# Attention and two feed-forward layers in one kernel: another order for the first loads and the first weight conversions

## The chip, the cores and the metric

The kernel runs on one core of one Trainium2 chip. The metric is the time of one execution on the device in microseconds (us). The kernel before was run three times: 1001.72 us in the median, 1000.77 to 1002.63.

## What is computed

There are N = 6016 tokens of C = 256 channels. The attention works across channels: queries and keys are normalised over the token axis, the scores are a 256 x 256 matrix summed over all tokens, and the softmax of it is applied to the values. Two feed-forward layers with DFF = 2048 follow.

```python
qn = q / (np.linalg.norm(q, axis=1, keepdims=True) + 1e-06)
kn = k / (np.linalg.norm(k, axis=1, keepdims=True) + 1e-06)
s = kn.transpose(0, 2, 1) @ qn / tau
a = softmax(s)
x = (v @ a).reshape(N, C)
h = x @ w_in1;  x = (relu(h) ** 2) @ w_out1
h = x @ w_in2;  out = np.maximum(0.01 * h, h) @ w_out2
```

So all of q and k has to be read before the softmax, and nothing of the feed-forward layers can start until the softmax is there.

## The kernel before

**The head (lines 237 to 507).** The 47 tiles of 128 tokens form 12 blocks (`tiles`, line 237): blocks 0 to 10 have four tiles, block 11 has three. `load_qk(n)` (line 331) loads one block of q and one of k into one buffer of five (`AHEAD`, line 240); `PIECES` (line 238) says in how many pieces: block 0 in four, blocks 1 to 3 in two, the others in one. All loads are issued by SyncE's queue (SP), except the keys of block 0, which ScalarE's queue issues (line 338).

The loop over the blocks (line 365) does this for block n, and each engine takes its own part in the order in which the lines stand, since the head runs under a manual schedule (line 322):

- ScalarE squares the block (line 371), then takes what lies in its list of later steps (line 374); after block 11 it also loads a table (line 373).
- VectorE adds the squares to `acc` (line 376). After block 11 it reduces `acc` to `sums_` (lines 378 to 380). Then it takes its list of later steps (line 381).
- TensorE multiplies q and k into the scores `sT` (line 386), 16 rows of the trace for a block of four tiles. Before the last two tiles it runs `norm_sums` (line 384), matmuls that read `sums_` and write `pn`.
- `run(steps[0], ...)` (line 393) takes steps of a weight conversion, and the next block, n + 5, is loaded (line 395).

After the loop the softmax follows: square roots of `pn` (line 437), small VectorE operations (440 to 446), scaling and transposing the scores (450 to 459), maxima and exponentials (470 to 474), transposes (478). TensorE multiplies the result into the first block of `w_in1` (`fold(0)`, line 497), and the first layer begins (line 704).

**A weight conversion.** A weight arrives as a 512 KB block of 64-bit words (`Unit.load`, line 131, three buffers `wst`). `converted` (line 294) turns it into a high and a low float: `scaled` (ScalarE, line 143), `shifted`, `sign`, `high` (VectorE, lines 146, 149, 153), `round` (ScalarE, line 192), `low` (VectorE, line 110). The first `next` puts `scaled` into ScalarE's list; each of the next three issues one VectorE step; the last of them puts `round` into ScalarE's list, and `low` goes to VectorE's list one block later.

In the kernel before, `first_i[0]` (block 0 of `w_in1`) is loaded behind block 3 (line 343) and converted around blocks 2 to 4 (`STEPS`, line 354). `first_i[1]` is loaded behind block 11 (line 397) and converted between the loop and the softmax (lines 433 to 452). `first_o` (block 0 of `w_out1`) is loaded behind the values and `tau` (line 401), and its conversion is a task of the plan below.

**The rest (lines 510 to 1913).** Everything behind the softmax is a list of tasks with costs and due times. `build` makes the tasks, `simulate` orders them with a model of the engines, and the plan whose TensorE ends first is written out. `convert` (line 1021) makes the tasks of a weight conversion; `CONV_BEGIN, CONV_END` (line 881) bound the stretch in which the weights of the second layer are converted; `FOLD_AFTER` (line 883) says behind which product of a unit the fold of the next one stands. The first four units of the first layer have a fixed order on TensorE (`PLAIN`, line 518).

Of the kernel before, what the change touches and what calls it, by code (L numbers as in the profile page):

```python
# [28 lines left out]
def attn_moe_moe2(  # L29
# [12 lines left out]
    nc = tc.nc  # L42
# [3 lines left out]
    T = N // P  # L46
# [188 lines left out]


    tiles = [(t0, min(G, T - t0)) for t0 in range(0, T, G)]
    PIECES = {0: ((0, 1), (1, 1), (2, 1), (3, 1)), **{n: ((0, 2), (2, 2)) for n in (1, 2, 3)}}
    NS = len(tiles)
    AHEAD = 5  # L240
    sT = [bank("ab"[j], f"sT{j}") for j in range(KC)]
# [52 lines left out]
    def converted(units):  # L294

        for u in units:
            later[ACT].append(u.scaled)
            yield
            for step in (u.shifted, u.sign, u.high):
                step()  # L300
                if step == u.high:
                    later[ACT].append(u.round)
                    later[ACT].append(lambda u=u: later[DVE].append(u.low))
                yield

    def run(steps, n):
        for _ in range(n):
            next(steps, None)

    first_i = [Unit("i", 1, g) for g in range(2)]  # L310
    first_o = Unit("o", 1, 0)
    others = [Unit(kind, 1, g) for k in range(1, NG) for kind, g in (("i", k + 1), ("o", k)) if g < NG]
    with (
# [17 lines left out]
        def load_qk(n):  # L331
            t = qk[n] = att4.tile([P, 2, G, C], F32, tag="qk", name="qk")
            for i, m in pieces(n):

                t0 = (tiles[n][0] + i) * P
                for a, x in enumerate((q, k)):
                    src = x[0][t0 : t0 + m * P, :].rearrange("(p g) c -> p g c", g=m)
                    (nc.scalar if a and n == 0 else nc.sync).dma_start(t[:, a, i : i + m], src)  # L338

        for n in range(AHEAD):  # L340
            load_qk(n)
            if n == 3:
                first_i[0].load()
        tiny = small[:, 6, 0:1]
        nc.vector.memset(tiny, 1e-36)
        nc.scalar.activation(small[:, 7, 0:1], ones, AF.Square)
# [2 lines left out]

        for _ in range(6):  # L350
            nc.tensor.matmul(warm[:, :P], zeros, zeros, start=True, stop=True)
        steps = [converted([u]) for u in first_i]

        STEPS = {2: 1, 3: 3}

        def norm_sums():

# [7 lines left out]
        for n, (t0, g) in enumerate(tiles):  # L365
            t = qk.pop(n)
            last_tile = n == NS - 1

            sq = att2.tile([P, 2, G, C], F32, tag="sq", name="sq") if n else acc
            for i, m in pieces(n):  # L370
                nc.scalar.activation(part(sq, i, m), part(t, i, m), AF.Square)
            if last_tile:
                nc.scalar.activation(small[:, 7, 0:1], ones, AF.Sqrt)
            flush(ACT)
            if n:
                tt(part(acc, 0, g), part(acc, 0, g), part(sq, 0, g), op=ALU.add)
            if last_tile:
                tt(part(acc, 0, 2), part(acc, 0, 2), part(acc, 2, 2), op=ALU.add)
                tt(sums_[:, :C], acc[:, 0, 0], acc[:, 0, 1], op=ALU.add)
                tt(ordered(sums_[:, C:]), in_order(acc[:, 1, 0]), in_order(acc[:, 1, 1]), op=ALU.add)  # L380
            flush(DVE)
            for i in range(g):
                if last_tile and i == g - 2:
                    norm_sums()
                for j in range(KC):
                    nc.tensor.matmul(  # L386
                        sT[j][:, :C],
                        t[:, 0, i, j * P : (j + 1) * P],
                        t[:, 1, i],
                        start=n == 0 and i == 0,  # L390
                        stop=last_tile and i == g - 1,
                    )
            run(steps[0], STEPS.get(n, 0))
            if n + AHEAD < NS:
                load_qk(n + AHEAD)
            elif n + AHEAD == NS:
                first_i[1].load()
                load_first_v(0)
                load_first_v(1)
                nc.sync.dma_start(tau_sb, tau.partition_broadcast(P))  # L400
                first_o.load()
                others[0].load()

        xa, xb = x_tile(2, 1, 0), x_tile(1, 1, 0)

# [24 lines left out]

        nc.vector.reciprocal(rtau, tau_sb)

        run(steps[1], 1)
        flush(ACT)
        run(steps[1], 2)
        y, m, z, r = (small[:, i] for i in range(4))
        nc.scalar.activation(y, pn[:, :4], AF.Sqrt, bias=tiny, scale=0.25)
        nc.scalar.activation(small[:, 7, 0:1], ones, AF.Exp)
# [10 lines left out]
        sTs = [att.tile([P, C], F32, name=f"sTs{j}") for j in range(KC)]  # L449
        ts(ordered(sTs[0]), in_order(sT[0][:, :C]), r[:, 0:1], rtau, op0=ALU.mult, op1=ALU.mult)  # L450
        nc.scalar.activation(ordered(sTs[1]), in_order(sT[1][:, :C]), AF.Copy, scale=rq1)
        run(steps[1], 1)
        others[1].load()
        s = [bank("e", "s0"), bank("y3", "s1")]
        x_transpose(0, 0, "y1")
        x_transpose(1, 0, "y2", range(2))
# [421 lines left out]
    TAIL = 12  # L878
    TURNS = 14
    FIRST_MIXED = min([p for L, p in GROUPS if L == 1], default=0)  # L880
    CONV_BEGIN, CONV_END = 1.4, 4
    N0 = 4
    FOLD_AFTER = "F1"
    LOAD = 22
    VDUE = 30, 60
    SEED_GAPS = 1, 0
# [100 lines left out]
    def build(base):  # L987
# [6 lines left out]
        wi_b, wo_b, x_b, g_b, c_b, o_b, v_b = {}, {}, {}, {}, {}, {}, {}  # L994
        low_of, x_ready = {}, {}
        wi_ready, wo_ready = {}, {}
        stores = {}
        y_after = {}

        def T(*a, **k):  # L1000
            return Task(*a, **k)
# [15 lines left out]
        wst_b = {i: Buf("wst", 3, i - 10) for i in range(3)}  # L1017
# [3 lines left out]
        def convert(u, due, loaded=None, first=None, pace=4, begin=0):  # L1021
            L, g = u.L, u.g
            d = lambda i: due + i * pace
            blocks = u.blocks
            if loaded is None:
                w = Buf("wst", 3, d(-12))
                t = T("SP", "wst", d(-12), u.load, alloc=w, lat=LOAD, deps=[begin] if begin else (),
                      release=d(-12) - 60 if begin else 0)
                deps = [t]
            else:  # L1030
                w, deps = loaded, ()
            cm = Buf("cm", 2, d(0))
            t = T("ACT", 3.2, d(0), u.scaled, deps=deps, alloc=cm, uses=[w])
            t = T("DVE", 1.9, d(1), u.shifted, deps=[t], uses=[cm])
            t = T("DVE", 3, d(2), u.sign, deps=[t], uses=[w, cm])
            if blocks:
                raw_ = Buf("whl", 2, d(4))
                t = T("DVE", 3, d(4), u.high, deps=[t], alloc=raw_, uses=[w, cm])
                for i in range(4):
                    t = T("DVE", 1.1, d(4.2 + i / 10), lambda i=i: (sums if u.kind == "i" else out_sums)(u.x)[i](),  # L1040
                          deps=[t], uses=[raw_])
                to = Buf("wis", 1, d(5))
                t = T("ACT", 4.6, d(5), u.round, deps=[t], alloc=to, uses=[raw_])
                t = T("DVE", 5.2, d(6), u.low, deps=[t], uses=[raw_, to])
            else:
                t = T("DVE", 3, d(4), u.high, deps=[t], uses=[w, cm])
                if (u.kind, L) == ("o", 1):
                    to = wo_b[1, 0, g] = Buf("wo", 4, d(5))
                elif u.kind == "i":
                    to = whl_b[g] = Buf("whl", 2, d(5))  # L1050
                else:
                    to = Buf("whl", 2, d(5))
                t = T("ACT", 2.7, d(5), u.round, deps=[t], alloc=to, uses=[cm])
                t = T("DVE", 3, d(6), u.low, deps=[t], uses=[cm, to])
            if u.kind == "o" or L == 2:
                stores[u.kind, L, g] = T("SP", "wo" if L == 1 else "wi" if u.kind == "i" else "store", d(7), u.store, deps=[t], uses=[to], lat=LOAD)
            return t

        whl_done = {0: None, 1: None}
        for i, u in enumerate([first_o, *others]):  # L1060
            n = u.g - 1 if u.kind == "i" else u.g + 1
            m, at0 = in_pair0(n)
            due = at0(m["fold"] if u.kind == "i" else m["second"][u.g > 0][0])
            t = convert(u, due - 35 - (0 if i else 10), loaded=wst_b.get(i))
            if u.kind == "i":
                whl_done[u.g] = t
            else:
                wo_ready[1, 0, u.g] = t
# [36 lines left out]
        for n in range(N0):  # L1105
            L, p, g = units[n]
            w = WIDTH[p]
            m, at0 = in_pair0(n)
            if g + 1 == N0 < NG:
                fixed.append(fold_sums(n, at0(m["fold"])))  # L1110
            elif g + 1 < NG:
                pw = {}
                b = wi_b[1, 0, g + 1] = Buf("wi", 3, at0(m["fold"]))
                t = T("PE", 6.4, at0(m["fold"]), lambda g=g, pw=pw: pw.update(enumerate(fold(g + 1))),
                      deps=[whl_done[g + 1], *pw_after], alloc=b, uses=[whl_b[g + 1], eT_b])
# [12 lines left out]
            for i, (half, fb) in enumerate(((0, 0), (0, 1), (1, 0), (1, 1))):  # L1128
                tag = "abe"[(4 * n + i) % 3]
                if (n, i) == (0, 0):  # L1130
                    t = T("PE", 12, at0(0), plain_first_both, n, "ab", uses=[wi])
                    fixed.append(t)
                elif (n, i) != (0, 1):
                    t = T("PE", 6, at0(m["first"][i]), plain_first, n, half, fb, tag,
                          deps=[*bank_after.get(tag, ()), wi_ready[1, 0, g]], uses=[wi])
# [5 lines left out]
            for half in range(2):  # L1141
# [4 lines left out]
                t = T("ACT", 4.6, at0(m["cast"][half]), nonlinear, n, half, w, "cast", deps=[t], uses=[c], alloc=b)  # L1146
# [797 lines left out]
```

## Time and profile before

| what | value |
|---|---|
| median of three runs | 1001.72 us (1000.77 to 1002.63) |
| the profiled execution | 1002.93 us |
| its span, first to last instruction | 1001.1 us |
| TensorE (PE) busy | 994.6 us, 99% of the span |
| VectorE (DVE) busy | 901.4 us, 90% |
| ScalarE (ACT) busy | 804.4 us, 80% |
| DMA | 234.97 MB, mean 235 GB/s |

The profiled execution is one run of its own: it took 1.8 us more than its span, and 1.2 us more than the median of the runs. Times in the rows below are microseconds from the start of the span.

### The profile page before, as it was taken

What the parts mean: (1) busy time and instruction counts of PE and PEld (TensorE: products, weight loads), DVE (VectorE), ACT (ScalarE), POOL (GpSimd) and SP (SyncE); (2) the same over time, 40 slices, a digit from 0 to 9 for tenths busy, and PEclk for the clock granted to TensorE, in tenths of its full rate; (3) what the DMA queues carried; (4) which work ended last, traced back from release to release, by engine and by line L of the source; (5) the groups of instructions that cost most, each with busy time, mean ns of one, the idle gap of its engine ahead of it and who ended that gap; (6) DMA issues with size and microseconds to landing.
All of it is one profiled execution on the core that took longest, in us unless ns stands there. A gap on an engine that the chain in (4) does not pass through costs nothing.

```text
span 1001.1 us, 13148 instructions
## 1 busy us (share of the span) xinstructions
PE 994.6 (99%) x4528; PEld 837.3 (84%) x4528; DVE 901.4 (90%) x1314; ACT 804.4 (80%) x1184; POOL 0.7 (0%) x6
## 2 busy tenths in 40 slices
PE   9999999999999999999999999999999999999998
PEld 7888888887888888998888888888888888998887
DVE  4899999988988977999999999999999999998985
ACT  6799978877878777888898888779788788887773
POOL 0000000000000000000000000000000000000000
PEclk9999999999999999999999999999999999999999
DMA  9786559788978967965665665666577586676553
GB/s 339 281 253 205 200 193 287 266 308 296 332 284 294 318 249 265 316 219 206 223 209 200 229 215 202 201 217 226 172 219 233 182 239 227 210 233 220 195 143 84
DMA packets 160946, 234.97 MB, mean 235 GB/s; under 512 B 53232, under 2 KB 97264, under 8 KB 158576
## 3 DMA queue, kind: packets, MB, share of 16 engines
q1 hardware_dynamic: 160160, 233.48, 69.0%
q8 instruction: 36, 0.59, 0.2%
q10 hardware_dynamic: 720, 0.66, 0.2%
q14 instruction: 30, 0.25, 0.1%
HBM read 187.70 MB, written 46.40 MB: 234 GB/s over the span
## 4 chain that ended last, share of the span: by engine, by line
PE 97%; DMA 2%; DVE 0%; ACT 0%; ACTq 0%; issue 0%; SPq 0%
PE y L543 37%; PE ha L543 21%; PE hb L543 16%; PE yA L543 7%; PE yF L543 3%; PE hc L543 3%; PE sT L386 3%; PE he L543 2%; PE h L704 2%; PE pw L252 1%; DMA qk<-in_k_dram 1%; DMA qk<-in_q_dram 1%; PE y L587 0%; DVE o L552 0%; ACT e L472 0%; ACTq L338 0%
## 5 line engine op out<-in xcount | busy, mean ns | idle before, releaser
L543 PE MATMUL y<-g,wo 128*128 128x512 f32 (+1 forms) x1344 | 350.5, 387 | 0.0
L543 PEld LDWEIGHTS y<-g,wo 128*128 128x128 f32 x1344 | 252.1, 188 | 49.5 <-DVE wo L110 0.4
L543 PE MATMUL ha<-x,wi 128*128 128x512 f32 (+1 forms) x960 | 265.6, 385 | 0.0
L110 DVE TENSOR_TENSOR g<-c,g 128x1024 fp32r<-128x1024 f32 (+1 forms) x192 | 228.0, 1197 | 18.7 <-ACT g L674 13.9
L543 PEld LDWEIGHTS ha<-x,wi 128*128 128x128 f32 x960 | 180.0, 188 | 33.8 <-ACT c L1504 0.7
L543 PE MATMUL hb<-x,wi 128*128 128x512 f32 (+1 forms) x720 | 199.6, 386 | 0.1
L543 PEld LDWEIGHTS hb<-x,wi 128*128 128x128 f32 x720 | 134.3, 188 | 26.2 <-DVE c L550 1.7
L1612 DVE TENSOR_TENSOR c<-c 128x512 f32<-128x512 f32 (+1 forms) x208 | 139.9, 672 | 7.1 <-ACT c L691 1.2
L1587 ACT CAST g<-c 128x1024 fp32r<-128x1024 f32 (+1 forms) x104 | 105.2, 1023 | 5.1 <-PE y L543 2.4
L110 DVE TENSOR_TENSOR b<-c,b 128x512 fp32r<-128x512 f32 (+1 forms) x156 | 102.5, 668 | 2.0 <-ACT b L1605 1.7
L1605 ACT CAST b<-c 128x512 fp32r<-128x512 f32 (+1 forms) x156 | 93.1, 608 | 10.5 <-DVE c L1612 4.7
L681 ACT ACTIVATE c<-c 128x1024 f32<-128x1024 f32 (+1 forms) x96 | 100.0, 1043 | 1.5
L674 ACT CAST g<-c 128x1024 fp32r<-128x1024 f32 (+1 forms) x88 | 91.7, 1044 | 1.6
L1504 ACT COPY w<-ha 128x512 f32<-128x512 f32 (+1 forms) x80 | 46.2, 577 | 49.9 <-PE ha L543 49.6
L691 ACT ACTIVATE c<-c 128x512 f32<-128x512 f32 (+1 forms) x98 | 60.7, 621 | 8.8 <-DVE c L552 8.5
L1504 ACT COPY u<-ha 128x512 f32<-128x512 f32 (+1 forms) x80 | 46.0, 575 | 9.8 <-PE ha L543 6.9
L110 DVE TENSOR_TENSOR x<-xr,x 128x1024 fp32r<-128x1024 f32 (+3 forms) x47 | 49.1, 1051 | 0.6 <-ACT x L1261 0.6
L386 PE MATMUL sT<-qk 128*128 128x256 f32 x188 | 42.1, 382 | 1.4 <-DMA qk<-in_k_dram 1.3
L543 PE MATMUL yA<-g,wo 128*128 128x512 f32 (+1 forms) x156 | 42.9, 383 | 0.0
L543 PE MATMUL yF<-g,ws 128*128 128x512 f32 (+1 forms) x156 | 42.9, 383 | 0.0
L543 PE MATMUL y<-b,ws 128*128 128x512 f32 (+1 forms) x156 | 42.9, 383 | 0.0
L543 PE MATMUL y<-b,wo 128*128 128x512 f32 (+1 forms) x156 | 42.8, 383 | 0.0
(137 smaller groups left out, 1202.4 us busy)
## 6 DMA issues: line engine op xcount, KB each, us to landing
wi<-wi SPq DMA_DIRECT2D x88, 896.0 KB, 5.6
wo<-wo SPq DMA_DIRECT2D x84, 512.0 KB, 4.5
ws<-wo SPq DMA_DIRECT2D x120, 128.0 KB, 4.0
wst<-in_moe_w_in_dram SPq DMA_DIRECT2D x16, 512.0 KB, 6.0
wst<-in_moe_w_out_dram SPq DMA_DIRECT2D x16, 512.0 KB, 6.8
wi<-wis SPq DMA_DIRECT2D x8, 896.0 KB, 6.1
wo<-wis SPq DMA_DIRECT2D x7, 1024.0 KB, 7.6
wo<-wos SPq DMA_DIRECT2D x13, 512.0 KB, 5.8
```

The costliest lines, as they stand in the source:

```text
L110: tt(lo, x, raw(hi), op=ALU.subtract)
L252: nc.tensor.matmul(pw[:, i * 2 * P : (i + 1) * 2 * P], eT[:, a, j, i * P : (i + 1) * P], whl[g][:, b, j], start=t == 0 and (i == 0 or g == 0),
L386: nc.tensor.matmul(sT[j][:, :C], t[:, 0, i, j * P : (j + 1) * P], t[:, 1, i], start=n == 0 and i == 0, stop=last_tile and i == g - 1,)
L543: nc.tensor.matmul(ps, a[m], b[n], start=first and i == 0, stop=i == 2, skip_group_check=True)
L674: nc.scalar.copy(g_t[n, half][:, 0, :, :w], c)
L681: nc.scalar.activation(c, c, AF.Square)
L691: nc.scalar.activation(c, c, AF.Prelu, alpha=0.01)
L704: nc.tensor.matmul(h_t[n, half, fb][:, :w], a[i], b[j], start=start, stop=stop, skip_group_check=True)
L1504: nc.scalar.copy(to, h(0))
L1587: nc.scalar.copy(g_t[n, name][:, 0, :, :w], result(n, half, w))
L1605: nc.scalar.copy(b_t[n, name][:, 0, :w], c(half, fb))
L1612: tt(c(*to), c(*a), c(*b), op=ALU.subtract)
```

## The change

Keys of block 1 are issued by ScalarE's queue, and block 3 is loaded in one piece. The first weight block is loaded behind block 6, the second (`first_i[1]`) behind block 8, the third (`first_o`) behind block 10; each is converted around the blocks that come next, the last one's `high` behind block 10 and its `low` behind the sums. So `first_i[1]` is no longer converted between the loop and the softmax, and `first_o` no longer by a task of the plan, which only stores it. Weight blocks 4 to 6 (`others`) are loaded one step earlier each. Two settings of the plan differ.

```diff
-    PIECES = {0: ((0, 1), (1, 1), (2, 1), (3, 1)), **{n: ((0, 2), (2, 2)) for n in (1, 2, 3)}}
+    PIECES = {0: ((0, 1), (1, 1), (2, 1), (3, 1)), **{n: ((0, 2), (2, 2)) for n in (1, 2)}}
...
-                    (nc.scalar if a and n == 0 else nc.sync).dma_start(t[:, a, i : i + m], src)
+                    (nc.scalar if a and n <= 1 else nc.sync).dma_start(t[:, a, i : i + m], src)
 
         for n in range(AHEAD):
             load_qk(n)
-            if n == 3:
-                first_i[0].load()
...
-        steps = [converted([u]) for u in first_i]
-
-        STEPS = {2: 1, 3: 3}
+        head_units = [*first_i, first_o]
+        steps = [converted([u]) for u in head_units]
+        LOADS = {1: 0, 3: 1, 5: 2}
+        STEPS = {5: (0, 1), 6: (0, 3), 7: (1, 1), 8: (1, 3), 9: (2, 1), 10: (2, 3)}
...
-            run(steps[0], STEPS.get(n, 0))
+            if n in STEPS:
+                i, m = STEPS[n]
+                run(steps[i], m)
             if n + AHEAD < NS:
                 load_qk(n + AHEAD)
+                if n in LOADS:
+                    head_units[LOADS[n]].load()
             elif n + AHEAD == NS:
-                first_i[1].load()
                 load_first_v(0)
                 load_first_v(1)
                 nc.sync.dma_start(tau_sb, tau.partition_broadcast(P))
-                first_o.load()
                 others[0].load()
+            elif n + AHEAD == NS + 2:
+                others[1].load()
...
-        run(steps[1], 1)
         flush(ACT)
-        run(steps[1], 2)
...
-        run(steps[1], 1)
-        others[1].load()
+        others[2].load()
...
-    CONV_BEGIN, CONV_END = 1.4, 4
+    CONV_BEGIN, CONV_END = 1.2, 4.3
-    FOLD_AFTER = "F1"
+    FOLD_AFTER = "F2"
...
-        for i, u in enumerate([first_o, *others]):
+        wo_ready[1, 0, 0], wo_b[1, 0, 0] = None, Buf("wo", 4, -8)
+        stores["o", 1, 0] = T("SP", "wo", -5, first_o.store, uses=[wo_b[1, 0, 0]], lat=LOAD)
+        for i, u in enumerate(others):
...
-            t = convert(u, due - 35 - (0 if i else 10), loaded=wst_b.get(i))
+            t = convert(u, due - 35, loaded=wst_b.get(i))
```

## Rows read from the trace of the kernel before

**Rows 1.** The page: engines, granted clock by slice, shares of the chain that ended last.

```profile
PE 994.6 (99%) x4528; PEld 837.3 (84%) x4528; DVE 901.4 (90%) x1314; ACT 804.4 (80%) x1184; POOL 0.7 (0%) x6
...
PEclk9999999999999999999999999999999999999999
...
PE 97%; DMA 2%; DVE 0%; ACT 0%; ACTq 0%; issue 0%; SPq 0%
```

**Rows 2.** Busy time by stretch (us, PE, PEld, DVE, ACT, POOL, PEclk, DMA share, GB/s).

```profile
57.50:157.50 100.00, 100.00 (x475) 83.81 (x474) 95.62 (x154) 87.36 (x130) 0.00 (x0) 1.00 0.67 223
```

**Rows 3.** TensorE's timeline: start, us, operation, count, idle before and releaser.

```profile
1.08 2.93 PE L351 MATMUL warm<-zeros 128*128 128x128 f32 x12 [1.08 <-DVE small L345]
...
8.57 1.97 PE L386 MATMUL sT<-qk 128*128 128x256 f32 x8 [0.66 <-DMA qk<-in_k_dram]
10.87 8.87 PE L386 MATMUL sT<-qk 128*128 128x256 f32 x40 [0.34 <-DMA qk<-in_k_dram]
20.05 25.28 PE L386 MATMUL sT<-qk 128*128 128x256 f32 x116 [0.30 <-DMA qk<-in_k_dram]
45.16 0.95 PE L360 MATMUL pn<-ones,sums 128*128 128x1 f32 x8
45.97 1.97 PE L386 MATMUL sT<-qk 128*128 128x256 f32 x8
...
52.95 3.01 PE L704 MATMUL h<-x,wi 128*128 128x512 f32 x12
55.98 1.70 PE L252 MATMUL pw<-whl,eT 128*128 128x256 f32 x12
57.52 8.35 PE L704 MATMUL h<-x,wi 128*128 128x512 f32 x36
```

**Rows 4.** VectorE's timeline, from the first conversion to the first layer.

```profile
19.48 0.42 DVE L146 TENSOR_SCALAR cm<-cm 128x512 uint32<-128x512 uint32 x1
...
20.67 0.69 DVE L153 SCALAR_TENSOR_TENSOR cm<-wst,cm 128x512 uint32<-128x512 uint32 x1
...
24.17 0.69 DVE L110 TENSOR_TENSOR whl<-cm,whl 128x512 fp32r<-128x512 f32 x1
24.77 4.69 DVE L376 TENSOR_TENSOR acc<-acc,sq 128x2048 f32<-128x2048 f32 x2
...
33.24 2.29 DVE L376 TENSOR_TENSOR acc<-acc,sq 128x2048 f32<-128x2048 f32 x1 [0.28 <-ACT sq L371]
...
38.37 4.15 DVE L376 TENSOR_TENSOR acc<-acc,sq 128x2048 f32<-128x2048 f32 x2 [0.32 <-ACT sq L371]
42.56 1.23 DVE L378 TENSOR_TENSOR acc<-acc 128x1024 f32<-128x1024 f32 x1
...
44.16 0.42 DVE L380 TENSOR_TENSOR sums<-acc 128x256 f32<-128x256 f32 x1
...
54.04 0.68 DVE L110 TENSOR_TENSOR whl<-cm,whl 128x512 fp32r<-128x512 f32 x1
54.64 1.28 DVE L110 TENSOR_TENSOR x<-x,x 128x512 fp32r<-128x512 f32 x2
```

**Rows 5.** ScalarE's timeline: its squares, and one `scaled` step of a conversion.

```profile
8.52 1.06 ACT L371 ACTIVATE sq<-qk 128x1024 f32<-128x1024 f32 x1 [1.30 <-DMA qk<-in_k_dram]
...
17.37 0.69 ACT L143 ACTIVATE cm<-wst 128x512 f32<-128x512 f32 x1
...
25.14 1.91 ACT L371 ACTIVATE sq<-qk 128x2048 f32<-128x2048 f32 x1 [0.68 <-DMA qk<-in_k_dram]
28.73 1.91 ACT L371 ACTIVATE sq<-qk 128x2048 f32<-128x2048 f32 x1 [1.67 <-DMA qk<-in_k_dram]
31.30 1.91 ACT L371 ACTIVATE sq<-qk 128x2048 f32<-128x2048 f32 x1 [0.66 <-DMA qk<-in_k_dram]
...
36.42 3.42 ACT L371 ACTIVATE sq<-qk 128x2048 f32<-128x2048 f32 x2 [0.70 <-DMA qk<-in_k_dram]
```

**Rows 6.** SyncE's queue: the issue of the first keys of block 1.

```profile
3.98 0.43 SPq L338 DMA_DIRECT2D qk<-in_k_dram  x1
```

## The prediction

> **What bounds the kernel now.** I read the page first. TensorE is busy for 99% of the span and makes 97% of the chain that ended last; the granted clock is full in every slice [rows 1]. Then the busy time by stretch: behind the head TensorE is busy for 100.00 of 100.00 us [rows 2]. The number of its rows does not change, so nothing can be won there; time can only be lost. What is left is the head, up to the first layer at 52.95 us, and I read it engine by engine.
>
> TensorE waits three times for the keys: 0.66 us for the first half of block 1, 0.34 for the second, 0.30 for block 4; from 20.05 it runs without a gap to `pn` at 45.16 [rows 3]. `pn` needs the sums. VectorE ends them at 44.16 + 0.42 = 44.58 [rows 4], only 0.58 us before TensorE asks for them. So a second chain runs beside TensorE's, nearly as long: load, square, add, reduce. At its end VectorE decides: from 38.37 its two last additions and the three reductions stand without a gap. Behind `pn` everything up to the first layer is one chain of short steps; when `pn` moves, it all moves.
>
> **The change, part by part.**
>
> *Loads.* In place of one weight block ahead of block 4 there are none; one stands ahead of block 7, two ahead of block 9, three ahead of block 11. A token block is two transfers of 512 KB and the squares of blocks 7 and 8 start 28.73 and 31.30, each as soon as the keys are there [rows 5]: 2.57 us per block, so 1.28 for a weight block. Blocks 7 and 8 have as much ahead of them as before, block 9 and 10 have 1.28 us more, block 11 2.56.
>
> *Queues.* SP loses four issues before block 4 (two keys of block 1, two halves of block 3) at 0.43 us each [rows 6], ScalarE's queue gets two. For this ScalarE starts its squares up to 1 or 2 us later; it waits 1.30 us ahead of block 1 [rows 5], which covers that, and if not, the first addition is late by the rest. What earlier issue buys for the landings lies between nothing (the DMA engines move all they can) and the three waits of TensorE together, 1.30 us. I take 0.4, about one issue, since the transfers already follow each other closely. The gain in TensorE's own waits is then about 0.4 + 0.30; but TensorE would only reach `pn` sooner, and it counts only if the sums are there.
>
> *Conversions.* This is the part that decides. The three VectorE steps of a conversion take 20.67 + 0.69 - 19.48 = 1.88 us, `low` 24.77 - 24.17 = 0.60 [rows 4]. Before, one conversion stood between the additions, and two stood behind the sums. Now the steps stand between the additions: 1.88 behind block 6, 0.60 behind 7, 1.88 behind 8, 0.60 behind 9, 1.88 behind 10; the third `low` stands behind the sums. VectorE takes them in this order, so each delays the next addition unless VectorE would have waited there. ScalarE's 0.69 (`scaled`) and about 0.6 (`round`) per conversion lie beside its waits of 0.6 to 1.7 us per block [rows 5]; if that cover goes, the squares become late, but VectorE is later still.
>
> I follow VectorE. Block 7 lands at about 28.7 - 0.4 = 28.3, its square ends at 30.25, its addition (2.29) at 32.55, the first `low` at 33.15. Block 8 is squared by 32.8, so its addition starts at 33.15 (before: 33.24 [rows 4]). From there to the end of the sums: three additions 6.87, two conversions 3.76, one `low` 0.60, the addition of block 11 4.15 - 2.29 = 1.86, the reductions 44.58 - 42.52 = 2.06 [rows 4]. That is 15.15 us: 48.3. The inputs come in time: block 9 is squared by about 36.7 and wanted at 37.3, block 10 by 39.2 and wanted at 40.2, block 11 by 42.0 and wanted at 44.4. Before, the same stretch took 44.58 - 33.24 = 11.34 with 0.5 of waiting in it.
>
> So `pn` starts at about 48.35 and not at 45.16: **3.2 us later**. TensorE, done with its rows at about 44.5, stands still for nearly 4 us, and its won waits are swallowed.
>
> *Behind `pn`.* The exponentials are reached at most 0.05 us sooner, since VectorE's and ScalarE's steps of the second conversion stood mostly in waits. Then the second `pw` (55.98) starts when VectorE's last `x` ends (54.64 + 1.28 = 55.92), with a `low` of 0.68 ahead of it [rows 4]. That `low` is gone; the 12 rows of TensorE ahead of `pw` end at 52.95 + 12 x 8.35 / 36 = 55.73 at the latest [rows 3], so 0.25 to 0.4 comes back. I take 0.35. What is late next there is TensorE itself.
>
> *The plan.* One conversion fewer, a store earlier, the window of the second layer's conversions wider, the fold one product later. All of it lies under a full TensorE [rows 2], so I cost it at nothing: no gain is possible, and a late weight or bank would show as idle TensorE. The bounds are 0 and about 1 us lost.
>
> **The sum**: +3.2 - 0.05 - 0.35 = +2.8 us. In the profiled execution: its span of 1001.1 us to 1003.9, its own time of 1002.93 to 1005.7. That execution is 1.2 us above the median of the runs; against the median the forecast is 1001.72 + 2.8 = **1004.5 us**. 0.2%, or 2.0 us, is about what a measurement of this kernel can tell from no change.
>
> Ends of the sum: block 7 landed 28.73 - 25.14 = 3.59 us behind block 6 and not 2.57 [rows 5]; if that 1.0 us does not come again and the queues give 1.3 in place of 0.4, the sums end 1.9 us earlier and the time is 1002.6. With nothing from the queues and some loss to ScalarE's late start or the plan it is 1005.3.
>
> **The rivals.**
>
> *TensorE's clock falls while it waits.* The 12 rows of 128 columns at the start take 2.93 us [rows 3], 0.24 each, where rows of 256 columns take 25.28 / 116 = 0.218 later: half the pace, which is 1.2 GHz against 2.4, after TensorE had done nothing. In the head before no wait is longer than 0.66 us; now one of nearly 4 us stands there. If the clock falls in it, `pn`, the eight rows of scores behind it (1.97 us [rows 3]) and part of the softmax run at half pace. The rows at the start stayed slow for about 2.7 us; with two to three such stretches on the path at half pace some 2.5 us are lost: 1007.0. Against it: the wait is short, and the clock has not moved in any slice [rows 1].
> The Trainium skill, "TensorE: Matmul & The Clock Gate", Part 1, says that an idle TensorE is put back to half clock and has to be busy for a while to get the full clock again; no row here shows it falling. By that rule the time would be that of this rival, without it that of the sum.
>
> *VectorE's waits take the conversions in: no measurable change.* Place: the additions of blocks 6 to 8. VectorE waited before some of its additions (0.28 and 0.32 us in the rows shown). If the landings of blocks 6 and 7 gain more than 1.2 us, the first conversion is done before block 7 is squared and the addition of block 8 starts at 32.3 or sooner. From there on less than 2.0 us is lost: about 1003.0. For it: the loads ahead of block 4 are fewer and larger. Against it: the same amount of data lies ahead of blocks 7 and 8 as before, and behind block 8 VectorE has 15.15 us of work without a wait whatever the loads do.
>
> *The conversions cost nothing and the loads' gain stays: faster.* If VectorE came to the sums by 44 us, TensorE would keep 0.30 and up to 1.0 of its waits and the 0.35: 1000.2. For it only that the order on VectorE would have to be another than the code's; the steps of the one conversion before stand exactly behind block 3's addition, at 19.48 [rows 4], as the code has them.
>
> **How the numbers follow.** The forecast 52%, its own range 1002.6 to 1005.3; the clock 18%; no measurable change 22%; faster 8%. Slower by over 0.2% needs 1003.7: most of the forecast's share (44%) and the clock's 18% make 62%; within 0.2%: 22% and 8% of the forecast's share make 30%; faster 8%. The range for 8 in 10 leaves out the faster case and the end of the clock's: 1002.3 to 1007.3.
>
> **What would show it.** In the new profile: the additions of blocks 9 and 11 start right behind a conversion's `high`, without a wait; `sums` end near 48.3; `pn` is released by VectorE and starts near 48.35; TensorE is idle before it for over 3 us; the second `pw` starts without a wait; TensorE is busy for 100 of 100 us behind the head. The forecast is wrong if `pn` starts before 46.5, if VectorE waits before the additions of blocks 9 to 11, if the rows of scores behind `pn` take twice their time (the clock), or if TensorE is idle in the plan.

## The result and the profile after

The changed kernel takes **1007.83 us** in the median of six runs (1006.07 to 1008.95), the kernel before 1001.65 in the runs beside them. The ratio is 1.006, 95% interval 1.0047 to 1.0073: 6.2 us slower. The forecast was 1004.5 with a range up to 1007.3, so the direction is right and the size is not. The profiled run is the fastest of the six, 1006.07 us with a span of 1004.3; it is 3.2 us longer than the span of before, 1001.1 us, which is itself that of a run 1.2 us above its median. The six spans and mean granted clocks are 1004.3 (1.000), 1006.1 (0.998), 1005.9 (0.998), 1006.6 (0.996), 1005.1 (0.998), 1007.1 (0.996). So two losses have to be found: one that the profiled run shows, and one that came with a lower clock in the five others.

TensorE's timeline of the changed kernel, as in [rows 3]:

```profile
8.94 35.66 PE L385 MATMUL sT<-qk 128*128 128x256 f32 x164 [0.89 <-DMA qk<-in_k_dram]
46.19 1.05 PE L359 MATMUL pn<-ones,sums 128*128 128x1 f32 x8 [1.58 <-DVE sums L378]
47.10 1.97 PE L385 MATMUL sT<-qk 128*128 128x256 f32 x8
...
54.39 3.01 PE L704 MATMUL h<-x,wi 128*128 128x512 f32 x12
57.24 1.59 PE L252 MATMUL pw<-whl,eT 128*128 128x256 f32 x12
```

The keys now make TensorE wait once and not three times; then it waits 1.58 us for the sums, by VectorE, as forecast, though not for the nearly 4 us that were forecast. VectorE's timeline, as in [rows 4]:

```profile
31.87 2.29 DVE L375 TENSOR_TENSOR acc<-acc,sq 128x2048 f32<-128x2048 f32 x1
34.08 0.42 DVE L146 TENSOR_SCALAR cm<-cm 128x512 uint32<-128x512 uint32 x1
...
35.87 2.29 DVE L375 TENSOR_TENSOR acc<-acc,sq 128x2048 f32<-128x2048 f32 x1
38.07 0.68 DVE L110 TENSOR_TENSOR whl<-cm,whl 128x512 fp32r<-128x512 f32 x1
38.67 2.28 DVE L375 TENSOR_TENSOR acc<-acc,sq 128x2048 f32<-128x2048 f32 x1
40.87 0.42 DVE L146 TENSOR_SCALAR cm<-cm 128x512 uint32<-128x512 uint32 x1
...
42.66 1.75 DVE L375 TENSOR_TENSOR acc<-acc,sq 128x1536 f32<-128x1536 f32 x1
...
46.05 0.42 DVE L379 TENSOR_TENSOR sums<-acc 128x256 f32<-128x256 f32 x1
```

No row from the addition of block 8 (31.87) to the end of the sums (46.05 + 0.42) has a wait ahead of it: 14.6 us, where the prediction had 15.15.

The first layer starts 54.39 - 52.95 = 1.44 us later than in [rows 3], the second `pw` 1.26. That is less than half of the 3.2 us. The rest lies farther back. [Rows 2] show the stretch from 57.5 to 157.5 us alone; the two of the kernel before that matter here were as full:

```profile
257.50:357.50 100.00, 100.00 (x442) 82.54 (x441) 87.94 (x141) 79.13 (x102) 0.00 (x0) 1.00 0.83 299
...
457.50:557.50 100.00, 100.00 (x446) 83.31 (x445) 94.39 (x130) 82.40 (x119) 0.00 (x0) 1.00 0.64 221
```

The changed kernel's busy time by stretch, columns as in [rows 2]:

```profile
160.00:260.00 100.00, 99.92 (x440) 81.77 (x439) 89.69 (x146) 80.53 (x105) 0.00 (x0) 1.00 0.85 292
260.00:360.00 100.00, 99.39 (x439) 82.01 (x438) 87.63 (x142) 77.27 (x100) 0.00 (x0) 1.00 0.84 293
360.00:460.00 100.00, 99.80 (x472) 88.23 (x471) 86.07 (x130) 81.79 (x120) 0.00 (x0) 1.00 0.76 254
460.00:560.00 100.00, 99.29 (x442) 82.45 (x441) 91.47 (x125) 81.28 (x117) 0.00 (x0) 1.00 0.62 217
```

The busy times fall short of 100 us by 0.08, 0.61, 0.20 and 0.71: 1.6 us together, of the 3.2 - 1.26 = 1.9 that are to be found. The two largest, from the timeline of the same profile (rows of ScalarE, TensorE, VectorE and TensorE):

```profile
280.83 0.67 ACT L143 ACTIVATE cm<-wst 128x512 f32<-128x512 f32 x1 [2.66 <-DMA wst<-in_moe_w_in_dram]
...
285.64 0.96 PE L543 MATMUL ha<-x,wi 128*128 128x512 f32 x3 [0.61 <-ACT c L1506]
...
466.99 1.23 DVE L1272 TENSOR_TENSOR xr<-xr 128x1024 f32<-128x1024 f32 x1 [1.47 <-DMA xr<-x]
...
470.01 0.96 PE L543 MATMUL hb<-x,wi 128*128 128x512 f32 x3 [0.71 <-DVE c L550]
```

ScalarE stood 2.66 us in front of the conversion of a weight that had not landed; the copies behind it in its queue were late, and TensorE waited for one of them. At 467 it is VectorE that stood in front of the next inputs. In both, one engine waits in its fixed order for a transfer, and TensorE for that engine.

A second profile of the changed kernel:

> The changed kernel once more, for a profile of an ordinary run (the first was its fastest). Theory: span 1005 to 1007, pn between 46.2 and 47.1 behind a wait of 1.6 to 2.7 us, waits of TensorE behind the head of 2 us or more together, each behind a transfer that lands late, and a mean clock of 0.996 to 0.998, lost either behind pn (eight score rows in about 3 us) or behind the longest wait in the plan.

It took 1009.44 us, span 1007.7, mean clock 0.996: past the 1005 to 1007 that was expected, and longer than each of the six runs. VectorE's addition of block 8, then TensorE's timeline:

```profile
33.10 2.28 DVE L375 TENSOR_TENSOR acc<-acc,sq 128x2048 f32<-128x2048 f32 x1
...
47.42 1.87 PE L359 MATMUL pn<-ones,sums 128*128 128x1 f32 x8 [2.29 <-DVE sums L378]
49.15 3.76 PE L385 MATMUL sT<-qk 128*128 128x256 f32 x8
52.70 1.45 PE L425 MATMUL x<-ident,v_in_order 128*128 128x128 f32 x6
...
58.81 3.01 PE L704 MATMUL h<-x,wi 128*128 128x512 f32 x12
```

Its busy time from 40 to 60 us, columns as in [rows 2]:

```profile
40.00:60.00 20.00, 16.97 (x81) 14.29 (x80) 14.62 (x33) 12.24 (x24) 0.00 (x0) 0.83 0.28 97
```

Here the clock fell in the wait for the sums: behind it the eight score rows take 3.76 us, where [rows 3] have 1.97, and the granted clock of the stretch is 0.83 of full, so part of it ran at 1.2 GHz. The first layer starts at 58.81, 4.4 us later than in the profiled run above; 1.2 of it are the later sums (47.42 against 46.19), 3.2 the clock. TensorE's waits behind the head are there again, 0.95 us between 460 and 560 us, but they are 1.1 us in all and not the 2 us or more that were expected.

Where each loss lies can be read from the start of the first layer. From there to the end of the span it is 1001.1 - 52.95 = 948.2 us in the profile of before, 949.9 in the first of the changed kernel and 948.9 in the second. So of the second one's 6.6 us over before 5.9 lie in the head, its clock included, and 0.7 behind it; in the first it is 1.4 and 1.8.

### The profile page after: what moved, and what is told of

The parts are those of the page before. It is cut to its first block, busy times and chain, and to the rows that moved or that the text cites. A ratio compares the mean times of both kernels' runs of the same rounds, so it can differ in the third digit from the quotient of the medians.

```text
span 1004.3 us, 13138 instructions
## 1 busy us (share of the span) xinstructions
PE 994.8 (99%) x4528; PEld 837.7 (83%) x4528; DVE 902.9 (90%) x1314; ACT 804.0 (80%) x1183; POOL 0.7 (0%) x6
## 4 chain that ended last, share of the span: by engine, by line
PE 92%; DMA 3%; ACT 2%; DVE 2%; issue 1%; SPq 0%; ACTq 0%
PE y L543 35%; PE ha L543 21%; PE hb L543 15%; PE yA L543 7%; PE yF L543 3%; PE hc L543 3%; PE he L543 2%; PE h L704 2%; DMA qk<-in_k_dram 2%; PE pw L252 1%; PE sT L385 1%; DMA wst<-in_moe_w_in_dram 1%; DMA xr<-x 1%; DVE acc L375 1%; ACT c L681 1%
```

## The experiments

**The plan's settings alone.** The kernel before with

```diff
-    CONV_BEGIN, CONV_END = 1.4, 4
+    CONV_BEGIN, CONV_END = 1.2, 4.3
-    FOLD_AFTER = "F1"
+    FOLD_AFTER = "F2"
```

> The kernel before with the two plan settings of the change (CONV_BEGIN, CONV_END = 1.2, 4.3 and FOLD_AFTER = F2) and nothing else. Theory A (the settings make the idle TensorE that the changed kernel shows between 240 and 470 us): about 2 us slower, 1003.7 us, with TensorE waits of some 0.5 us each in that stretch, and the granted clock at 1.00. Theory B (the stalls come from the changed list of tasks, the third conversion gone from the plan): no difference, 1001.6 us. Either way the head is that of before: pn at 45.2 us, the first layer at 52.95.

1002.32 us against 1001.26; ratio 1.001, interval 1.0001 to 1.0019. TensorE's waits behind the head are there (0.56 us between 160 and 260 us, 0.69 between 360 and 460). The settings make stalls, but the run is only about 1 us longer, half of what theory A wanted. The head was not quite that of before: `pn` started at 44.47 and not near 45.2.

**The head alone, with the old settings.** The changed kernel with the two lines above turned back.

> The changed kernel with the plan settings of before (1.4, 4 and F1). Theory A (settings): the stalls of the plan are gone, only the head's loss is left: span 1002.3 us where the clock stays full; with the clock's loss in most runs a median of about 1005. Theory B (tasks): as the changed kernel, about 1007.8 us. The head should be that of the changed kernel: pn at 46.2, released by VectorE.

1008.65 us, ratio 1.008 (1.0067 to 1.0093): no faster than the whole change. TensorE waits 2.6 us for the sums and 1.9 us at one place between 160 and 260 us. All five runs have a clock of 0.996 to 0.998. Theory A falls: with the old settings the stalls stay. Theory B comes near (about 1007.8), but it wanted no loss from the settings alone, and they had one. Either change makes another order, and both orders lose. Which settings suit the changed list better is not shown: 1.008 and 1.006 have intervals that overlap.

**TensorE kept busy ahead of the sums.** The changed kernel with

```diff
                 if last_tile and i == g - 2:
+                    for _ in range(7):
+                        nc.tensor.matmul(warm[:, :P], zeros, zeros, start=True, stop=True)
                     norm_sums()
```

> The changed kernel with seven more matmuls of zeros (128 columns each, 1.5 us together, into the bank of the warm-up) ahead of norm_sums, so that TensorE works where it waited 1.58 us for the sums; they change no result. Theory C (the timed runs are longer than the profiled one because the clock falls in that wait): granted clock 1.000 in every run and a median of about 1006.1 us. Theory D (the clock falls somewhere else, or the extra time has another cause): about 1007.8 us and mean clocks of 0.996 to 0.998 as in the changed kernel.

1008.63 us, ratio 1.0068 (1.0055 to 1.008). The wait for the sums shrank to 0.34 us and the score rows behind it took 1.97. The clock was 1.000 in three of five runs, but these took 1006.27, 1007.34 and 1008.63 us. In the profiled run the clock fell elsewhere. Its busy time from 460 to 560 us:

```profile
460.00:560.00 100.00, 97.77 (x428) 81.04 (x427) 88.57 (x122) 79.80 (x115) 0.00 (x0) 0.98 0.60 209
```

TensorE lacks 2.2 us of work there, and the clock is 0.98. The list of waits of this stretch says why (total in us, times, longest):

```profile
DVE xr L1274 <- DMA xr<-x: 3.0, 1, 3.0
...
PE hb L545 <- DVE c L552: 2.2, 1, 2.2
```

VectorE stood 3.0 us in front of `xr`, where it had stood 1.47 in the first profile, and TensorE 2.2 us behind VectorE. So neither theory holds alone: the clock falls in the wait for the sums in the second profile above, and the stalls of the plan differ from run to run, by enough to hide what the clock gives back, and one of them is long enough for the clock to fall in it too.

**The third conversion behind the sums.** The changed kernel with its conversion taken out of the blocks:

```diff
-        STEPS = {..., 8: (1, 3), 9: (2, 1), 10: (2, 3)}
+        STEPS = {..., 8: (1, 3)}
...
+        run(steps[2], 1)
         flush(ACT)
+        run(steps[2], 2)
...
+        run(steps[2], 1)
         others[2].load()
```

> The changed kernel with the third conversion (first_o) taken out of the blocks: its steps stand behind the sums, where the kernel before had those of first_i[1]. If VectorE's work ahead of the sums decides, they end 1.85 us earlier, at 44.65 us, TensorE waits 0.2 us or less at pn, pn starts at 44.7, the first layer at 52.9 or a little earlier, and the clock stays at 1.000: with the stalls of the plan as in the changed kernel (2.0 us) about 1003.5 us. If the loads decide (block 11 lands later than before), pn stays near 46 us and little changes: 1007.

1004.89 us, ratio 1.0034 (1.0021 to 1.0047). TensorE's timeline:

```profile
45.05 1.05 PE L359 MATMUL pn<-ones,sums 128*128 128x1 f32 x8 [0.57 <-DVE sums L378]
...
52.94 3.04 PE L707 MATMUL h<-x,wi 128*128 128x512 f32 x12
```

The expected 44.7 and 1003.5 us were missed a little. The head is that of [rows 3] (45.16 and 52.95), the mean clock 1.000 in the profiled run. Yet the span is 1003.3, 2.2 us longer than the first one of before: all of that is the plan, whose waits are again behind transfers (2.5 us of ScalarE for a weight, 1.5 of VectorE for `xr`). VectorE decides when the sums end; moving 1.8 us of it away moved `pn` from 46.19 to 45.05, less than the step is long, as the addition of block 8 began 0.47 us later in this run (32.34 against 31.87).

**The new head with the order of before.** The plan is made with the old settings and with steps for `first_o` that do nothing, so that behind the head every instruction stands as before (counted from 64 us in the trace of before, every engine has the same instructions in the same order in both traces):

```diff
...
+    class Done:
+        kind, L, g, blocks = "o", 1, 0, False
+        scaled = shifted = sign = high = round = low = lambda self: None
+        def store(self):
+            first_o.store()
...
-        for i, u in enumerate(others):
+        for i, u in enumerate([Done(), *others]):
```

> The whole changed head, with the plan of before: the plan is made with the settings of before and with steps for first_o that do nothing, so that every instruction behind the head stands in the order of before. Theory P (the loss behind the head comes from the order of the new plan): no TensorE wait behind 60 us, only the head's loss of 1.2 us where the clock stays and about 3.4 where it falls: a median between 1002.4 and 1004.7 us. Theory H (the stalls behind the head come from the head ending later): stalls as in the changed kernel and about 1007.8 us.

1004.66 us, ratio 1.0032 (1.0021 to 1.0044). Busy time by stretch of the slowest run, span 1005.4:

```profile
40.00:60.00 20.00, 16.87 (x80) 14.19 (x79) 14.74 (x33) 12.46 (x24) 0.00 (x0) 0.83 0.16 59
...
160.00:260.00 100.00, 100.00 (x440) 81.91 (x439) 91.04 (x149) 81.94 (x108) 0.00 (x0) 1.00 0.86 293
260.00:360.00 100.00, 100.00 (x443) 82.84 (x442) 88.64 (x142) 79.61 (x104) 0.00 (x0) 1.00 0.83 299
...
460.00:560.00 100.00, 100.00 (x447) 83.62 (x446) 94.51 (x129) 83.80 (x120) 0.00 (x0) 1.00 0.63 220
```

Theory P holds: no wait of TensorE behind the head, though this head ended later than any other but that of the second profile above (first layer at 58.35, there 58.81). Theory H falls. TensorE waited 2.67 us for the sums here, and eight score rows took 3.76 us. Three runs had full clock and spans of 1001.9 to 1002.2, three 0.997 or 0.998 and 1003.4 to 1005.4; the spans of the runs of before beside them lie between 998.9 and 1001.4, most near 999.6. So **the head costs 2.4 us, and 2 us more when the clock falls**; 1.2 and 3.4 were expected, from a profile of before that lies above most of its runs.

The changed kernel differs from this variant in the plan alone: 1.006 / 1.0032 leaves 0.28%, or 2.8 us, to the new order; a part of it can be the clock's, which was lower in five of six runs there and in three of six here. The profiles agree on the order. From the first layer to the end it is 946.8 to 948.2 us in the seven profiles whose plan is that of before, wherever their head ends, and 948.9 to 955.7 in the seven with another order.

The head here and the whole loss of the variant above, 1.0032 x 1.0034 = 1.0066, also come near the 1.006 of the change; the second is that variant's plan, not the change's own, so that this is a fit of sizes and no proof.

**A wait of that length in the kernel before.** Two useless additions ahead of the reductions:

```diff
             if last_tile:
+                tt(part(sq, 0, 3), part(sq, 0, 3), part(sq, 0, 3), op=ALU.add)
+                tt(part(sq, 0, 1), part(sq, 0, 1), part(sq, 0, 1), op=ALU.add)
                 tt(part(acc, 0, 2), part(acc, 0, 2), part(acc, 2, 2), op=ALU.add)
```

> The kernel before with two useless additions on VectorE (1.75 and about 0.5 us, on squares that are no longer read) between the addition of block 11 and the reductions; loads, conversions and plan as before. The sums end near 46.85 us and TensorE waits 1.7 to 2.4 us at pn, as long as in the changed kernel and its variant without the settings. If a wait of that length at this place is enough to bring the clock down, some runs show a mean clock under 1.000 and slow score rows behind pn (3.1 us for eight, not 1.97), and the median is 1004 to 1005 us. If the clock needs more than that (the plan's stalls, or another load), all runs have 1.000 and the median is 1001.3 + 1.7 = 1003.0 us.

1003.86 us, ratio 1.0017 (1.0009 to 1.0026). In the profiled run TensorE waited 1.56 us:

```profile
46.22 1.05 PE L360 MATMUL pn<-ones,sums 128*128 128x1 f32 x8 [1.56 <-DVE sums L381]
```

and the clock stayed. Of eleven runs four had 0.998 and a median span of 1003.1 us, seven had 1.000 and 1000.6. So a wait made in this place, with loads and plan as before, is enough to bring the clock down in some runs, and the medians are then 2.5 us apart (the two groups overlap: one span at full clock is 1002.7, one of the others 1002.1). How long the wait was in the four is not recorded. None of the 54 runs of the kernel before beside the variants has a mean clock under 0.999. The median lies just under the branch that was expected for a falling clock.

**The new head, the old order, and TensorE kept busy.** The variant with the order of before, with ten of the matmuls of zeros.

> The changed head with the plan of before (as e6_old_plan, which had full clock in three of six runs, spans near 1002.0, and 0.997 or 0.998 in the other three, spans of 1003.4 to 1005.4) and ten matmuls of zeros ahead of norm_sums, 2.1 us in TensorE's wait for the sums; they change no result. If the clock falls because TensorE stands still there: 0.999 or 1.000 in every run, spans near 1002.0, a median of 1003.8 us. If it falls for another reason: half of the runs at 0.998 again, a median of about 1004.7 us.

1004.45 us, ratio 1.0034 (1.0023 to 1.0045). TensorE's timeline:

```profile
47.35 1.05 PE L359 MATMUL pn<-ones,sums 128*128 128x1 f32 x8 [0.20 <-DVE sums L378]
48.26 1.97 PE L387 MATMUL sT<-qk 128*128 128x256 f32 x8
```

Six of seven runs have 0.999 or 1.000 and spans of 1002.0 to 1002.8, one has 0.998 and 1005.0. One fall in seven against three in six points to the stillness ahead of `pn`, but the runs are few, and one fell all the same. The median is nearer to the branch of the other theory: it gains only 0.2 us on the variant without the matmuls, since at full clock these runs were some 0.5 us longer than its own; why is open. That the fall comes in this wait is shown by rows: the score rows right behind it are slow in the second profile of the change and in the variant with the old order, and have 1.97 us where the matmuls fill it.

**Two conversions among the blocks.** The kernel before with the changed loads, both blocks of `w_in1` converted among the token blocks, `first_o` and the order of the plan as before:

```diff
...
-        STEPS = {2: 1, 3: 3}
+        LOADS = {1: 0, 3: 1}
+        STEPS = {5: (0, 1), 6: (0, 3), 7: (1, 1), 8: (1, 3)}
...
```

> The plan of before, the changed loads of q and k, and two conversions among the blocks in place of three: first_i[0] loaded behind block 6, first_i[1] behind block 8, each converted as in the changed kernel; first_o stays where it was before (loaded behind the values, converted in the plan). VectorE has 1.88 us less ahead of the sums than in the changed kernel, so they end at about 44.6 us, pn starts between 44.6 and 45.1, and the second pw no longer waits (0.25 to 0.4 us): 1000.4 to 1001.0 us, clock 1.000. If the weight block that now stands ahead of block 11 decides instead, pn is at 45.5 to 46 and the time is 1001.5 to 1002.

1002.93 us, ratio 1.0015 (1.0006 to 1.0024): slower, past both branches. TensorE's timeline:

```profile
44.98 1.05 PE L359 MATMUL pn<-ones,sums 128*128 128x1 f32 x8 [0.35 <-DVE sums L378]
...
52.98 3.05 PE L703 MATMUL h<-x,wi 128*128 128x512 f32 x12
55.86 1.59 PE L252 MATMUL pw<-whl,eT 128*128 128x256 f32 x12
```

Two conversions are already enough to make `pn` wait; a head without them reached it at 44.47 (the settings' run) and 44.09 (the next one), though at 45.16 in [rows 3]. Against the next one the first layer starts 1.0 us later (52.98, there 52.00) and the span is 1.3 us longer; against [rows 3] the head is not later, so that where the 0.15% lie is not fully shown. The second `pw` comes 55.86 - 52.98 = 2.88 us behind the first layer and not 3.03 [rows 3], so the `low` ahead of it was worth 0.15.

**The loads alone.** The changed loads of q and k, the first conversion behind block 6, all else as before:

```diff
...
-        STEPS = {2: 1, 3: 3}
+        STEPS = {5: 1, 6: 3}
...
```

> The kernel before with the changed loads of q and k alone: keys of block 1 by ScalarE's queue, block 3 in one piece, first_i[0] loaded behind block 6 and converted there; the second and third conversion and the plan as before. VectorE has no more work ahead of the sums than before, so they end by 44 us, pn does not wait, and TensorE comes to it at 44.5: if this part of the change is worth what the waits for block 1 and 4 show, 0.2 to 0.7 us faster than before, 1000.8 to 1001.3 us. If the stretch from 160 to 360 us, where transfers fill 0.8 to 0.9 of the time, gives it back: no difference.

1001.18 us against 1001.3, ratio 1.0003 (0.9994 to 1.0012): no measurable difference, though `pn` starts without a wait at 44.09 and the first layer at 52.00.

**The kernel before, a second profile.**

> The kernel before once more, for a second profile. The first one's execution was 1.2 to 1.4 us above the median of all its runs, and its head reached pn at 45.16. If the head's loads make that difference, a run near the median shows pn at about 44.5 and the first layer at about 52.2, and small waits between 160 and 460 us give part of it back, as in the variants that keep its plan; the span is 999.3 to 1000.5.

It was again a run above the median (1002.86 us, span 1001.1, not the 999.3 to 1000.5 expected), with `pn` at 45.08 and 0.17 and 0.14 us of idle TensorE between 160 and 260 and between 360 and 460 us. So no profile shows the head of an ordinary run of before, and whether the loads' gain is given back later or ordinary runs of before reach `pn` as early stays open.

**The model's landings.**

```diff
-    LANDS = 14
+    LANDS = 24
```

> The changed kernel with one number of the planner's model raised: LANDS, the time from the end of a transfer's turn to its landing, from 14 to 24 of the planner's units (a unit is about 0.23 us). In the changed kernel ScalarE waits 2.66 us at 278 to 281 for a weight block that took 8.07 us, where the model reckons about 4.7; the work queued behind it makes TensorE wait. Theory M (the new order trusts landings that the chip does not keep): the stalls behind the head go, what is left is the head: 1002.5 to 1004.7 us. Rival (another cause, or the new order is worse elsewhere): 1006 us or more.

1014.85 us, ratio 1.0134 (1.0118 to 1.0149). Theory M as a cure falls. The waits for `wst` are gone from the list of waits, but TensorE's timeline has one long stall:

```profile
429.73 1.49 PE L543 MATMUL hb<-x,wi 128*128 128x448 f32 x3 [7.11 <-DVE c L550]
```

Another order, another weak place, and this one is no late transfer: from 422.6 us on, VectorE is busy for 6.1 of the 6.5 us ahead of the step that TensorE waits for, with work that stands ahead of it in its queue, and no engine waits 0.2 us for a transfer between 62 and 500 us. In the six other profiles with a new order TensorE's longest stall behind the head ends 3 to 5 us behind an engine's wait for a transfer. That these orders lose to late transfers is read from the traces and was not tested by itself; which number of the model would have to change was not found.

## Why the prediction was wrong

**VectorE's chain: the mechanism right, its length too long.** The conversions stand where the prediction put them, and from the addition of block 8 to the sums VectorE has no wait. But from the start of that addition to `pn` it is 14.3 us in each of the seven profiles with this head, where the forecast has 48.35 - 33.15 = 15.2: it added up full durations, and each operation starts a little before the one ahead of it is listed as ended (2.28 long, the next 2.20 later, 33.10 to 35.30 in the second profile); and `pn` is released by the first half of the sums (`sums L378` in its row, 46.19), not by the second, which ends at 46.47. And the addition of block 8, forecast for 33.15, started between 31.71 and 33.10. So `pn` came at 46.19 in the first profile, under the 46.5 that the prediction had named as a sign against it, and at 47.42 in the second; TensorE's wait was 1.58 to 2.67 us in the profiles without added matmuls, not over 3. Profile against profile `pn` moved by 1.0 to 2.3 us, not 3.2. That the head's loss between runs, 2.4 us at full clock, is near the forecast +2.8 is in part luck: it is measured against runs of before that are faster than the profile from which the forecast was worked out.

**Behind `pn`: two small terms off.** The exponentials did not come sooner: from `pn` to the first layer it is 54.39 - 46.19 = 8.20 us, before 52.95 - 45.16 = 7.79; why is open. And the `low` ahead of the second `pw` was worth 0.15 to 0.2, not 0.35. Together about 0.6 us.

**The plan: the step that failed.** "All of it lies under a full TensorE, so I cost it at nothing", with bounds of 0 and about 1 us lost. It cost 1.8 us in the first profile of the change, 2.2 us in the profile of the variant with the head on time and 0.34% over its runs, about 3.4 us; between the change and the variant with the order of before it is 2.8 us. [Rows 2] show one stretch, in which the changed kernel is full too (99.99 of 100 us from 60 to 160); the loss came later. TensorE was full behind the head because of that order, not because of the work: the same tasks ordered anew (settings alone) lose 1 us, with one task fewer and the old settings TensorE waits 1.9 us in one place. I treated a rebuilt order as an edit to the old one. A wider bound could have been read from the transfers, which fill 0.83 to 0.87 of the time between 157.5 and 357.5 us in the kernel before: where an engine comes to one that has not landed it stands still, with everything queued behind it, 2.66 us in the first profile.

**The clock: a rival that belonged in the sum.** It had 18% as a case of its own at 1007.0. The mean clock was lower in five of the six runs of the change, and the fall comes on top of the head's loss, in some runs and not in others; so it is a term with a chance, not another outcome. The price of 2.5 us was right in size: 2.1 to 2.5 between runs of the same kernel. In single profiles with the fall, the way from `pn` to the first layer is longer by 1.7 to 3.2 us (9.87 to 11.39 against 8.20). The Trainium skill, "TensorE: Matmul & The Clock Gate", Part 1, says that an idle TensorE drops to half clock and gets the full one back by sustained work. The trace of the second profile agrees: 0.83 in the stretch from 40 to 60 us, 1.00 from 60 to 160.

**The rivals on the other side.** The one in which the waits take the conversions in, about 1003.0, had its condition fulfilled in the first profile: the addition of block 8 started at 31.87, before 32.3, and `pn` was only 1.0 us late. Its time did not come, since the plan lost 1.8 us more; in the second profile, with 33.10, the condition was not there. The faster one fell: the order on VectorE was the code's. Head, plan and clock add up to a time outside the range: the head lost about what was forecast, and the other two, which stood at nothing in the sum, came on top of it in most runs. The range had been built as if only one of them could go wrong.

## What to carry to other kernels

Work moved out of a latency chain into a "busy" stage has to be added to the second-longest chain of that stage, queue by queue; here three conversions between VectorE's additions made these the chain on which everything waits. If a change alters the input of a scheduler, its cost is that of a new order, and it can be told apart from the edit by making the old order with empty steps. And a wait of TensorE of 2 us in a kernel that has none is to be priced with the clock.

## What was not expected of the hardware

The clock fell behind waits of 2.29 us (second profile of the change) and 2.67 us (the variant with the old order), and it fell in four of eleven runs of a kernel whose profiled run waited 1.56 us and kept it: the same program loses it in one run and not in the next. In those two profiles eight score rows took 3.76 us in place of 1.97; runs with the fall were 2.1 to 2.5 us longer in the median than runs of the same kernel without.
